# One-bank PSUM tiles in two feed-forward layers, and a planner whose lengths are distances between starts

## The chip, the cores and the metric

The kernel runs on one core of a Trainium2 chip. The metric is the device time of one execution in microseconds (us). Before the change the median of three runs is 803.41 us (802.49 to 804.92).

## The reference

Attention over 2 batches of 8 heads, 768 positions of 64 elements, in which a query sees only the keys that fall into its own hash bucket (signs of six projections). Its output, 1536 tokens of 512, goes through two feed-forward layers:

```python
attn_out = _attn_ref(q, k, v, proj)                      # softmax(mask(q k^T / 8)) v
x = attn_out.transpose(0, 2, 1, 3).reshape(1536, 512)
h = x @ w_in;  x = (h - tanh(h)) @ w_out                 # 512 -> 2048 -> 512
g = x @ w_gate                                           # 512 -> 1536
return (g * sigmoid(g) * (x @ w_val)) @ w_out2           # 1536 -> 512
```

All inputs are float32.

## The kernel before

**Precision and tiling.** Every operand of a matmul is split into a high and a low part (`split_g`, `split_w`, `x_split`), and three products of parts make one product: a *product* or an *output group* is an operation of six matmuls on TensorE (PE). The tokens go in two halves of 768 (`sb` 0 and 1), and a half in two blocks of 384 columns (`TB`).

**Seven products per unit.** A unit (`products`, L818) multiplies one pair of 128-row blocks of a weight matrix with one half of the tokens by a scheme of Strassen's kind: seven products in place of eight, P0 to P6 below, in the order of the table `PRODUCTS` (L808). Products accumulate in PSUM *banks*; a bank holds 512 float32 per partition and the core has eight. A unit uses both banks of a tile `s_t[z]` of shape [128, 2, 512] (z alternates from unit to unit), and a third bank out of a ring of four (`RING`, L813), which are the two banks of the tile `t`, also [128, 2, 512], and the one-bank tiles `x` and `h`. In the unit's order:

- P0 writes bank 0 of `s`; ScalarE (ACT) copies it out (`snap`, L830).
- P1 writes bank 1 of `s`; ACT copies it out.
- P2 writes the ring's bank; VectorE (DVE) adds the first copy (`add`, L833), and the activation follows.
- P3 adds to bank 0; ACT copies it out.
- P4 adds to bank 1; DVE adds the last copy into the bank (L833), ACT takes tanh or sigmoid (L791, L798), DVE works on (`tt`, L779), and in two of the three kinds of unit ACT and DVE make the high and the low part from that bank (L784, L779).
- P5 adds to bank 0; DVE reads it (L833).
- P6 adds to bank 0; activation and split follow.

Units are interleaved: the last products of one stand between the first of the next. Between products stand output groups (`out_group`, L882; matmuls L904), each into the ring's next bank; ACT or DVE copies the result out (L914, L915, L917, L928, L933), and for three or four results together GpSimd (POOL) issues a transfer that adds them to an accumulator (L941 in SBUF, L950 in memory).

**Weights.** They arrive as 64-bit words through two raw buffers (L271, SyncE's queue), are converted by three DVE operations per chunk (L273, L276, L279), combined (L305, L307) and split (L285, L287, L322, L324).

**Order of the work.** The order is not the program's: `Plan` (L65) holds each operation with its possible engines and a length on each, the keys that it reads and writes, a due time and a latency. `Plan.order` is a list scheduler: an engine that is free takes the ready operation with the earliest due time; an operation with two engines goes to the second when that one is free and `alt` allows. What depends on an operation becomes ready at its end plus `LAT` = 0.14 us (PE 0.25, transfers their own `lat`). Lengths of operations that were declared after the attention are multiplied by `SAFE` = 1.05. POOL and DVE operations with `port=BOTH` exclude each other. The resulting order is emitted, engine by engine, once (L1013 to the end of the function). The planner's keys are per bank: `("s", z, 0)` and `("s", z, 1)` are different things to it, as are `("t", 0)` and `("t", 1)`.

**Waits.** The tile layer below the kernel follows who touches which *tile* and puts in the semaphore waits. For the two-bank tiles of the kernel before it treats the tile as one: an access to one bank waits for earlier accesses of other engines to the other bank.

**Stages.** Attention fills the span to about 240 us, with first products of the layers in its last part; layer 1 (8 pairs of blocks) lasts to about 530 us, layer 2 (6 pairs, gate and value) to the end. In the attention the two-bank tiles are used whole: `s` for scores of 768 keys (L653, L662, L664), `t` for six transposes (L682, L688).

Of the kernel before, what the change touches and what calls it, by code (L numbers as in the profile page):

```python
# [21 lines left out]
TB = 384  # L22
# [42 lines left out]
class Plan:  # L65
# [120 lines left out]
def lsh_attention_moe_kernel(ctx: ExitStack, tc: tile.TileContext, qT, kT, vP, proj, cst, wts, out):  # L186
# [96 lines left out]
    def split_w(dst, src, rk, wk, n, due, late=False):  # L283
        hi, lo = dst
        op({"ACT": 0.19 + n / 1175}, lambda e: e.activation(out=hi, in_=src, func=ACTF.Copy),  # L285
           r=rk, w=[wk + (0,)], due=due, late=late)
# [31 lines left out]
    def declare_out(name, f, due, after):  # L318
        wk = ring("wo", NWO)
        convert(order_c[name, f], f_t, [("f", 0)], due - OLEAD, after)  # L320
        hi, lo = wo_t[wk[1]][:, 0, :], wo_t[wk[1]][:, 1, :]
        op({"ACT": 0.63}, lambda e: e.activation(out=hi, in_=f_t, func=ACTF.Copy),  # L322
           r=[("f", 0)], w=[wk + (0,)], due=due - 6)
# [454 lines left out]
    def tt(dst, dk, a, ak, b, bk, alu, due, port):  # L778
        op({"DVE": dve(TB), "POOL": pool(TB)} if port else {"DVE": 0.56}, lambda e: e.tensor_tensor(out=dst, in0=a, in1=b, op=alu),  # L779
           r=[ak, bk], w=dk, due=due, alt=ALT, port=BOTH * port)  # L780

    def split_g(key, src, sk, due, psum):
        (hi, hk, h1), (lo, lk, l1) = g_slot(), g_slot()
        op({"ACT": 0.52}, lambda g: g.activation(out=hi, in_=src, func=ACTF.Copy), r=[sk], w=[hk] + h1, due=due)  # L784
        tt(lo, [lk] + l1, src, sk, hi.bitcast(F32), hk, ALU.subtract, due + 0.6, not psum)
        gh[key] = hi, lo, [hk, lk]


    def block_tanh(key, src, sk, due, psum, keep, spare=None):
        t, tk, t1 = spare or t_slot(1)  # L790
        op({"ACT": 0.51}, lambda e: e.activation(out=t, in_=src, func=ACTF.Tanh), r=[sk], w=[tk] + t1, due=due)  # L791
        d, dk = (src, sk) if keep else (t, tk)
        tt(d, [dk], src, sk, t, tk, ALU.subtract, due + 0.6, not psum)
        split_g(key, d, dk, due + 1.2, keep and psum)

    def block_silu(key, src, sk, due, psum, keep, spare=None):
        t, tk, t1 = t_slot(2)
        op({"ACT": 0.51}, lambda e: e.activation(out=t, in_=src, func=ACTF.Sigmoid), r=[sk], w=[tk] + t1, due=due)  # L798
        tt(t, [tk], src, sk, t, tk, ALU.mult, due + 0.6, not psum)
# [12 lines left out]

    RING = [(("t", 0), t_t[0][:, 0, :]), (("t", 1), t_t[0][:, 1, :]), (("x", 0), x_t[0]), (("h", 0), h_t[0])]  # L813

    def bank_slot():
        return RING[ring("bank", len(RING))[1]]

    def products(name, i, sb):  # L818
# [5 lines left out]
        bkeys = [("s", z, 0), None, ("s", z, 1)]  # L824
        banks = [s_t[z][:, 0, 0:TB], None, s_t[z][:, 1, 0:TB]]
        (c0, k0, f0), (c1, k1, f1), (c2, k2, f2) = c_slot(), c_slot(), c_slot()
        block = {"in": block_tanh, "gate": block_silu, "val": block_val}[name]

        def snap(dst, dk, bank, bk, due):
            op({"ACT": 0.49}, lambda e: e.activation(out=dst, in_=bank, func=ACTF.Copy), r=[bk], w=dk, due=due)  # L830

        def add(dst, dk, bank, bk, c, ck, due):
            op({"DVE": 0.56}, lambda e: e.tensor_tensor(out=dst, in0=bank, in1=c, op=ALU.add), r=[bk, ck], w=[dk], due=due)  # L833

        def product(n):
            xn, wn, bi, first = PRODUCTS[n]
            if bi == 1:
                bkeys[1], b = bank_slot()
                banks[1] = b[:, 0:TB]
            bank, bk = banks[bi], bkeys[bi]  # L840
# [5 lines left out]
            def mm(e):  # L846
                m = 0
                for k in range(2):
                    for wpart, xpart in terms:
                        e.matmul(  # L850
                            out=bank, lhsT=w[:, wpart, wi * 256 + k * 128:wi * 256 + k * 128 + 128],
                            rhs=x_at(sb, xn, xpart, k), start=first and m == 0, stop=m == 5, skip_group_check=True,
# [29 lines left out]
    def out_group(layer, i, sb, j):  # L882
# [8 lines left out]
        gs = [gh[layer, i, sb, t, f] for f in range(2)]  # L891
        k, ps = bank_slot()
        ps = ps[:, 0:size]

        def mm(e):
            c = 0
            for f in range(2):
                w = wo_t[wks[f][1]]
                for wpart, gpart in terms:
                    if layer == 1:  # L900
                        lhs, rhs = w[:, wpart, m * 128:m * 128 + 128], gs[f][gpart]
                    else:
                        lhs, rhs = gs[f][gpart][:, m * 128:m * 128 + 128], w[:, wpart, :]
                    e.matmul(out=ps, lhsT=lhs, rhs=rhs, start=c == 0, stop=c == 5)  # L904
                    c += 1
# [5 lines left out]
        if layer == 1 and i in (0, NP1 - 1):  # L911
            if i == 0:
                op({"DVE": dve(TB), "ACT": 0.5}, lambda g:
                   g.activation(out=acc_at(sb, j), in_=ps, func=ACTF.Copy) if g is nc.scalar else  # L914
                   g.tensor_copy(acc_at(sb, j), ps), r=[k], w=[("acc", sb, j)], due=e, late=True)  # L915
            else:
                op({"DVE": 0.57}, lambda g: g.tensor_tensor(  # L917
                    out=acc_at(sb, j), in0=ps, in1=acc_at(sb, j), op=ALU.add,
                ), r=[k, ("acc", sb, j)], w=[("acc", sb, j)], due=e, late=True)
        elif layer == 2 and i == NP2 - 1:  # L920
# [6 lines left out]
            at_, key = stages["last"][m]  # L927
            op({"DVE": dve(DM)}, lambda g: g.tensor_tensor(out=at_(), in0=ps, in1=at_(), op=ALU.add), r=[k, key], w=[key], due=e)  # L928
            op({"SP": 0.5}, lambda g: g.dma_start(out=out[sb * S + j * 128:sb * S + j * 128 + 128, :], in_=at_()), r=[key], w=[], due=e)
        else:  # L930
            at_, key, first = stage(layer, m)
            op({"ACT": 0.18 + size / 1200, "DVE": dve(size)}, lambda g, at_=at_:
               g.activation(out=at_(), in_=ps, func=ACTF.Copy) if g is nc.scalar else g.tensor_copy(at_(), ps),  # L933
               r=[k], w=[key] + first, due=e, late=layer == 2, alt=EALT)
            if m == 0:
                stages[layer, "at"] = at_
            if m == n - 1:
                at_ = stages[layer, "at"]
                keys = [key[:3] + (c,) for c in range(n)]
                if layer == 1:  # L940
                    op({"POOL": 1.0}, lambda g, at_=at_: g.dma_start(out=acc_at(sb, 4 * t, 4), in_=at_(4), accum_op=ALU.add),  # L941
                       r=keys + aks, w=aks, due=e + 1, lat=5.0, late=True)
                else:
# [5 lines left out]
                    else:  # L949
                        op({"POOL": 1.0}, lambda g, at_=at_: g.dma_start(out=o, in_=src(at_), accum_op=ALU.add),  # L950
                           r=keys + [ok], w=[ok], due=e + 1, lat=5.0)
        if layer == 1 and i == NP1 - 1 and j == 7:
# [128 lines left out]
```

## Time and profile before

| | |
|---|---|
| median of three runs | 803.41 us |
| the profiled execution | 803.86 us, span 802.1 us |
| PE, matmuls | 766.6 us busy, 96% of the span |
| PE, weight loads (beside matmuls) | 661.5 us, 82% |
| DVE | 589.4 us, 73% |
| ACT | 466.8 us, 58% |
| POOL | 359.7 us, 45% |
| granted TensorE clock | 1.00 in every slice |
| transfers | 104.23 MB, mean 130 GB/s |

A matmul's row is longer than the time to the next matmul, because matmuls are pipelined; how fast PE goes is read from how long a run of matmuls takes as a whole. A weight load (PEld) belongs to each matmul and is issued by the same queue, so its waits are PE's waits.

### The profile page before, as it was taken

Reading aid. Unit: us, or ns where it says so; the run is one execution under the profiler, and the core shown is the slowest. Engines: PE = TensorE matmul, PEld = TensorE weight load, DVE = VectorE, ACT = ScalarE, POOL = GpSimd, SP = SyncE. Lnnn points to the kernel's source line nnn. Section 1 sums busy time; section 2 is a strip of 40 time slices with the busy share of each in tenths; the row PEclk is TensorE's granted clock in tenths of the full one; section 3 lists DMA queues with packets and bytes.
Section 4 is the critical chain, followed back from the end, with each engine's and each line's share of the span. In section 5 each row is a group of like instructions: output and inputs, shape, how many; then the busy total and the mean of one; then the engine's idle time right before and its main releaser. Section 6 shows DMA issues by size and latency. Waiting matters only on the chain.

```text
span 802.1 us, 12309 instructions
## 1 busy us (share of the span) xinstructions
PE 766.6 (96%) x4332; PEld 661.5 (82%) x4332; DVE 589.4 (73%) x1038; ACT 466.8 (58%) x906; POOL 359.7 (45%) x384
## 2 busy tenths in 40 slices
PE   5999999999999999999999999989989999999997
PEld 3766666666668889999999999989979898989996
DVE  6877777787698966786777668777765876877444
ACT  4787787786666754666545545554544455555530
POOL 4655567744475341343323454735245532344121
PEclk9999999999999999999999999999999999999999
DMA  7655444553222143777776761324327567666675
GB/s 213 161 131 139 109 133 115 124 134 74 73 66 93 53 117 94 165 189 177 178 171 161 157 142 47 86 79 158 120 73 149 128 150 158 121 155 132 119 167 187
DMA packets 38717, 104.23 MB, mean 130 GB/s; under 512 B 4704, under 2 KB 10080, under 8 KB 38656
## 3 DMA queue, kind: packets, MB, share of 16 engines
q1 hardware_dynamic: 28288, 71.06, 29.0%
q0 software_dynamic: 9904, 31.59, 22.9%
q10 hardware_dynamic: 464, 0.80, 0.4%
q8 instruction: 34, 0.56, 0.3%
q14 instruction: 27, 0.22, 0.1%
HBM read 49.17 MB, written 18.87 MB: 85 GB/s over the span
## 4 chain that ended last, share of the span: by engine, by line
PE 76%; DVE 11%; DMA 4%; ACT 3%; issue 3%; POOL 2%; SPq 0%; DVEq 0%; ACTq 0%; POOLq 0%
PE s L850 26%; PE t L904 13%; PE x L706 7%; PE t L682 7%; PE s L653 7%; PE h L904 6%; PE x L904 4%; DMA raw<-in_w 3%; DVE m L662 2%; PE x L850 2%; PE t L850 1%; ACT ct L664 1%; DMA acc<-ct 1%; DVE ct L779 1%; DVE op L779 1%
## 5 line engine op out<-in xcount | busy, mean ns | idle before, releaser
L850 PE MATMUL s<-x,wi 128*128 128x384 f32 x1200 | 235.1, 337 | 6.4 <-DVE ct L833 2.1
L850 PEld LDWEIGHTS s<-x,wi 128*128 128x128 f32 x1200 | 209.1, 188 | 18.6 <-DVE ct L833 4.0
L662 DVE TENSOR_REDUCE m<-s 128x1 f32<-128x768 f32 x96 | 89.3, 951 | 29.3 <-PE s L653 28.7
L671 POOL TENSOR_SCALAR ct<-ct,r 128x768 f32<-128x768 f32 x96 | 94.1, 988 | 33.4 <-DVE r L670 29.2
L664 ACT ACTIVATE ct<-s,m 128x768 f32<-128x768 f32 x96 | 85.8, 896 | 20.6 <-DVE m L662 19.7
L653 PE MATMUL s<-op 128*128 128x384 f32 x384 | 88.9, 366 | 6.7 <-ACT ct L664 6.4
L830 ACT ACTIVATE ct<-s 128x384 f32<-128x384 f32 x120 | 58.1, 490 | 58.6 <-PE s L850 58.1
L682 PEld LDWEIGHTS t<-csb,ct 128*128 128x128 f32 x576 | 64.4, 141 | 31.2 <-issue 18.7
L682 PE MATMUL t<-csb,ct 128*128 128x128 f32 x576 | 81.6, 278 | 5.2 <-POOL ct L671 1.7
L904 PE MATMUL t<-op,wo 128*128 128x384 f32 x384 | 77.0, 338 | 4.8 <-DVE acc L917 1.5
L653 PEld LDWEIGHTS s<-op 128*128 128x128 f32 x384 | 66.5, 195 | 17.5 <-ACT ct L664 15.3
L904 PEld LDWEIGHTS t<-op,wo 128*128 128x128 f32 x384 | 66.9, 188 | 7.8 <-DVE acc L917 2.1
L706 PE MATMUL x<-pt,v 128*64 128x384 f32 x384 | 69.0, 495 | 0.0
L287 POOL TENSOR_TENSOR wi<-fs,wi 128x512 fp32r<-128x512 f32 (+1 forms) x37 | 57.1, 1553 | 24.1 <-ACT wi L285 18.0
L904 PE MATMUL t<-wo,op 128*128 128x512 f32 x264 | 67.5, 393 | 0.0
L688 ACT ACTIVATE pt<-t 128x768 f32<-128x768 f32 x59 | 47.9, 811 | 29.7 <-PE t L682 28.6
L324 POOL TENSOR_TENSOR wo<-f,wo 128x512 fp32r<-128x512 f32 x17 | 22.4, 1316 | 75.1 <-ACT wo L322 70.9
L904 PEld LDWEIGHTS t<-wo,op 128*128 128x128 f32 x264 | 48.9, 188 | 8.2
L850 PE MATMUL s<-op,wi 128*128 128x384 f32 x240 | 48.2, 337 | 1.8 <-DVE ct L779 1.6
L706 PEld LDWEIGHTS x<-pt,v 128*64 128x64 f32 x384 | 24.7, 136 | 28.4 <-issue 28.4
L285 ACT ACTIVATE wi<-fs 128x512 fp32r<-128x512 f32 (+1 forms) x60 | 41.5, 701 | 10.4 <-DVE fs L305 4.0
L779 POOL TENSOR_TENSOR ct<-ct 128x384 f32<-128x384 f32 x20 | 20.6, 1029 | 59.9 <-ACT ct L791 31.0
(164 smaller groups left out, 1378.8 us busy)
## 6 DMA issues: line engine op xcount, KB each, us to landing
raw<-in_w SPq DMA_DIRECT2D x68, 512.0 KB, 3.9
acc<-ct POOLq DMA_DIRECT2D x24, 768.0 KB, 6.0
out<-acc POOLq DMA_DIRECT2D x16, 768.0 KB, 7.8
op<-raw SPq DMA_DIRECT2D x42, 192.0 KB, 3.0
op<-f SPq DMA_DIRECT2D x56, 96.0 KB, 2.5
v<-in_v SPq DMA_DIRECT2D x8, 384.0 KB, 3.2
out<-acc SPq DMA_DIRECT2D x4, 768.0 KB, 4.1
acc<-out SPq DMA_DIRECT2D x4, 768.0 KB, 4.5
```

What stands on the lines that cost most here:

```text
L285: op({"ACT": 0.19 + n / 1175}, lambda e: e.activation(out=hi, in_=src, func=ACTF.Copy), r=rk, w=[wk + (0,)], due=due, late=late)
L287: op({"POOL": pool(n), "DVE": dve(n)}, lambda e: e.tensor_tensor(out=lo, in0=src, in1=hi.bitcast(F32), op=ALU.subtract), r=rk + [wk + (0,) ...
L653: g.matmul(out=s[:, kh, 0:TB], lhsT=(b, a)[first][:, q0], rhs=ks[kh][0 if first else 1], start=first, stop=not first,)
L662: op({"DVE": 0.87}, lambda g: g.tensor_reduce(out=m, in_=sv, axis=AX.XY, op=ALU.max, negate=True), r=[sk + (0,), sk + (1,)], w=[mk], due=d ...
L664: op({"ACT": 0.9}, lambda g: g.activation(out=p.rearrange("p (a b) -> p a b", a=2), in_=sv, func=ACTF.Exp, bias=m, accum_out=sm), r=[sk + ...
L671: op({"POOL": 0.95}, lambda g: g.tensor_scalar(out=p, in0=p, scalar1=r, scalar2=1.0, op0=ALU.mult, op1=ALU.mult), r=[pk, rk], w=[pk], due= ...
L682: g.transpose(out=t_t[0][:, kt // 3, c0:c0 + 128], in_=p[:, kt * 128:(kt + 1) * 128], identity=ident)
L688: op({"ACT": 0.75, "DVE": 0.87}, lambda g: g.activation(out=dst, in_=src, func=ACTF.Copy) if g is nc.scalar else g.tensor_copy(dst, src), ...
L706: g.matmul(out=x[r, :], lhsT=v[:, kt, r], rhs=pt_t[ptks[e][1]][:, kt, :], start=(kt == 0), stop=(kt == NKT - 1), tile_position=(0, 64 * e),)
L830: op({"ACT": 0.49}, lambda e: e.activation(out=dst, in_=bank, func=ACTF.Copy), r=[bk], w=dk, due=due)
L850: e.matmul(out=bank, lhsT=w[:, wpart, wi * 256 + k * 128:wi * 256 + k * 128 + 128], rhs=x_at(sb, xn, xpart, k), start=first and m == 0, st ...
L904: e.matmul(out=ps, lhsT=lhs, rhs=rhs, start=c == 0, stop=c == 5)
```

## The change

Three things change.

1. In the layers each of the six banks of `s` and `t` becomes a tile of its own. The attention still uses two-bank tiles. When the last operation of the attention that touches such a tile has been emitted, its pool is closed (`narrow`) and two tiles [128, 512] are opened in its place. Operations look their bank up when they are emitted (`bank_at`, `now`).
2. The planner's lengths become the distance from one operation's start to the next one's start on the same engine: for DVE (n+65)/960 us in place of (n+151)/960 - 0.01, for ACT 0.07 + n/1200 in place of figures from 0.49 to 0.52 us for 384 columns, for POOL 0.13 + n/457 in place of 0.16 + n/457, for the conversions 0.34 and 0.60 us in place of 0.43 and 0.69. `LAT`, `SAFE`, the due times and all other constants stay.
3. The accumulating transfers: in layer 1 POOL's issue 0.87 us in place of 1.0 and a latency of 6.0 us in place of 5.0, in layer 2 1.3 in place of 1.0 and 7.5 in place of 5.0.

`pool(n)` is also used by operations on the first batch's attention output, declared within the attention (384 columns: 0.970 in place of 1.000 us).

```diff
@@ Plan
+        self.banks = {}
 ...
+        self.banks[n] = {("t", 0) if k[0] == "t" else k[:2] for k in (*r, *w) if k[0] in ("s", "t")}
@@ lsh_attention_moe_kernel
-    s_t = tiles(ctx, "s", 2, [128, 2, 512], space=PSUM)
-    t_t = tiles(ctx, "t", 1, [128, 2, 512], space=PSUM)
...
-    late = {}
+    wide = {k: ExitStack() for k in (("t", 0), ("s", 0), ("s", 1))}
+    t_t = tiles(wide["t", 0], "t", 1, [128, 2, 512], space=PSUM)
+    s_t = [tiles(wide["s", z], "s%d" % z, 1, [128, 2, 512], space=PSUM, side=("left", "right")[z])[0] for z in range(2)]
+    late = {("x", 0): x_t[0], ("h", 0): h_t[0]}
...
-    W_TS, W_STT = 0.43, 0.69
+    W_TS, W_STT = 0.34, 0.6
...
     def pool(n):
-        return 0.16 + n / 457
+        return 0.13 + n / 457
     def dve(n):
-        return (n + 151) / 960 - 0.01
+        return (n + 65) / 960
+    def act(n):
+        return 0.07 + n / 1200
...
-        op({"ACT": 0.52}, lambda g: g.activation(out=hi, in_=src, func=ACTF.Copy), r=[sk], w=[hk] + h1, due=due)
+        op({"ACT": act(TB) + 0.03}, lambda g: g.activation(out=hi, in_=now(src), func=ACTF.Copy), r=[sk], w=[hk] + h1, due=due)
...
-        op({"ACT": 0.51}, lambda e: e.activation(out=t, in_=src, func=ACTF.Tanh), r=[sk], w=[tk] + t1, due=due)
+        op({"ACT": act(TB) + 0.02}, lambda e: e.activation(out=t, in_=now(src), func=ACTF.Tanh), r=[sk], w=[tk] + t1, due=due)
...
-    RING = [(("t", 0), t_t[0][:, 0, :]), (("t", 1), t_t[0][:, 1, :]), (("x", 0), x_t[0]), (("h", 0), h_t[0])]
+    RING = [("t", 0), ("t", 1), ("x", 0), ("h", 0)]
+    def bank_at(key, size):
+        return lambda: late[key][:, 0:size]
+    def now(ap):
+        return ap() if callable(ap) else ap
+    def narrow(key):
+        wide[key].close()
+        keys = [("t", 0), ("t", 1)] if key[0] == "t" else [key + (0,), key + (1,)]
+        for k in keys:
+            late[k] = tiles(ctx, "b%s%d%d" % (*key, k[-1]), 1, [128, 512], space=PSUM, side="right")[0]
...
-        banks = [s_t[z][:, 0, 0:TB], None, s_t[z][:, 1, 0:TB]]
+        banks = [bank_at(bkeys[0], TB), None, bank_at(bkeys[2], TB)]
...
-            op({"ACT": 0.49}, lambda e: e.activation(out=dst, in_=bank, func=ACTF.Copy), r=[bk], w=dk, due=due)
+            op({"ACT": act(TB)}, lambda e: e.activation(out=dst, in_=bank(), func=ACTF.Copy), r=[bk], w=dk, due=due)
...
-            op({"DVE": 0.56}, lambda e: e.tensor_tensor(out=dst, in0=bank, in1=c, op=ALU.add), r=[bk, ck], w=[dk], due=due)
+            op({"DVE": dve(TB) + 0.01}, lambda e: e.tensor_tensor(out=now(dst), in0=bank(), in1=c, op=ALU.add), r=[bk, ck], w=[dk], due=due)
...
-                    op({"POOL": 1.0}, lambda g, at_=at_: g.dma_start(out=acc_at(sb, 4 * t, 4), in_=at_(4), accum_op=ALU.add),
-                       r=keys + aks, w=aks, due=e + 1, lat=5.0, late=True)
+                    op({"POOL": 0.87}, lambda g, at_=at_: g.dma_start(out=acc_at(sb, 4 * t, 4), in_=at_(4), accum_op=ALU.add),
+                       r=keys + aks, w=aks, due=e + 1, lat=6.0, late=True)
...
     order, first_late = plan.order()
+    last = {}
+    for i, (n, e, _) in enumerate(order):
+        for key in plan.banks.get(n, ()) if n < plan.n_first else ():
+            last[key] = i
+    ends = {i: key for key, i in last.items()}
     with tc.manual_schedule():
-        for n, e, _ in order[:first_late]:
+        for i, (n, e, _) in enumerate(order[:first_late]):
             plan.ops[n][1](eng[e])
+            if i in ends:
+                narrow(ends[i])
```

The same pattern (a looked-up bank, `act(...)` or `dve(...)` as the length) is applied to the other layer operations in `split_w`, `declare_out`, `tt`, `block_silu` and `out_group`.

## Rows read from the trace of the kernel before

**Rows 1.** Page, part 1: engine, busy us (share of the span), instructions.
```profile
PE 766.6 (96%) x4332; PEld 661.5 (82%) x4332; DVE 589.4 (73%) x1038; ACT 466.8 (58%) x906; POOL 359.7 (45%) x384
```
**Rows 2.** Busy time by stretches: length, engines' busy us (instructions), granted clock, DMA, GB/s.
```profile
240.50:300.00 59.50, 56.97 (x326) 50.21 (x325) 49.56 (x77) 38.11 (x75) 28.27 (x23) 1.00 0.30 86
300.00:500.00 200.00, 197.70 (x1119) 193.23 (x1119) 146.81 (x262) 110.57 (x230) 72.57 (x65) 1.00 0.62 148
500.00:610.00 110.00, 104.03 (x551) 96.04 (x550) 79.91 (x141) 55.86 (x108) 56.81 (x46) 1.00 0.39 112
610.00:798.00 188.00, 185.75 (x953) 169.06 (x951) 126.55 (x223) 87.05 (x169) 62.21 (x54) 1.00 0.65 144
```
**Rows 3.** The chain that ended last, in order of time: start us, us, what.
```profile
311.11 2.08 PE t L904 x12
...
614.98 7.49 DMA raw<-in_w
...
787.30 2.73 PE t L904 x12
```
**Rows 4.** Waits of PE's weight loads, 240 to 802 us: us, times, longest.
```profile
PEld s L850 <- DVE ct L779: 4.5, 9, 1.0
PEld s L850 <- DVE ct L833: 4.0, 4, 1.9
PEld s L850 <- ACT ct L830: 3.4, 5, 1.1
PEld s L850 <- DVE op L779: 3.2, 3, 1.6
...
PEld t L904 <- DVE acc L917: 2.1, 2, 1.4
PEld s L850 <- ACT op L784: 1.9, 8, 0.2
PEld t L904 <- DVE op L779: 1.7, 2, 1.0
PEld t L904 <- ACT ct L791: 1.0, 1, 1.0
PEld t L904 <- ACT acc L914: 1.0, 1, 1.0
PEld s L850 <- DVE s L779: 0.9, 2, 0.5
PEld t L904 <- DVE t L779: 0.8, 1, 0.8
```
**Rows 5.** Timeline about 586 us: start, us, engine, line, operation [idle before <-releaser].
```profile
584.42 1.26 PE L850 MATMUL s<-x,wi 128*128 128x384 f32 x6
...
585.72 0.57 DVE L779 TENSOR_TENSOR s<-s,ct 128x384 f32<-128x384 f32 x1 [0.84 <-PE s L850]
586.32 0.56 DVE L833 TENSOR_TENSOR ct<-s,ct 128x384 f32<-128x384 f32 x1
...
587.43 0.56 DVE L779 TENSOR_TENSOR op<-s,op 128x384 fp32r<-128x384 f32 x1 [0.56 <-ACT op L784]
...
588.04 0.65 PEld L850 LDWEIGHTS s<-x,wi 128*128 128x128 f32 x4 [1.64 <-DVE op L779]
```
**Rows 6.** Timeline of DVE about 624 us, operations without idle time between them.
```profile
623.43 0.69 DVE L276 SCALAR_TENSOR_TENSOR fs<-raw,fs 128x512 uint32<-128x512 uint32 x1
...
624.03 0.55 DVE L779 TENSOR_TENSOR ct<-s,ct 128x384 f32<-128x384 f32 x1
...
624.50 0.55 DVE L833 TENSOR_TENSOR ct<-s,ct 128x384 f32<-128x384 f32 x1
```
**Rows 7.** Page, part 6: transfers' issues, count, KB each, us to landing.
```profile
raw<-in_w SPq DMA_DIRECT2D x68, 512.0 KB, 3.9
acc<-ct POOLq DMA_DIRECT2D x24, 768.0 KB, 6.0
out<-acc POOLq DMA_DIRECT2D x16, 768.0 KB, 7.8
```

More of the change, by code (lines that the diff above doesn't have):

```diff
@@ L284, in split_w @@
         hi, lo = dst
-        op({"ACT": 0.19 + n / 1175}, lambda e: e.activation(out=hi, in_=src, func=ACTF.Copy),
+        op({"ACT": act(n)}, lambda e: e.activation(out=hi, in_=src, func=ACTF.Copy),
            r=rk, w=[wk + (0,)], due=due, late=late)
@@ L321, in declare_out @@
         hi, lo = wo_t[wk[1]][:, 0, :], wo_t[wk[1]][:, 1, :]
-        op({"ACT": 0.63}, lambda e: e.activation(out=hi, in_=f_t, func=ACTF.Copy),
+        op({"ACT": act(512)}, lambda e: e.activation(out=hi, in_=f_t, func=ACTF.Copy),
            r=[("f", 0)], w=[wk + (0,)], due=due - 6)
@@ L778, in tt @@
     def tt(dst, dk, a, ak, b, bk, alu, due, port):
-        op({"DVE": dve(TB), "POOL": pool(TB)} if port else {"DVE": 0.56}, lambda e: e.tensor_tensor(out=dst, in0=a, in1=b, op=alu),
+        op({"DVE": dve(TB), "POOL": pool(TB)} if port else {"DVE": dve(TB) + 0.01}, lambda e: e.tensor_tensor(out=now(dst), in0=now(a), in1=b, op=alu),
            r=[ak, bk], w=dk, due=due, alt=ALT, port=BOTH * port)
@@ L797, in block_silu @@
         t, tk, t1 = t_slot(2)
-        op({"ACT": 0.51}, lambda e: e.activation(out=t, in_=src, func=ACTF.Sigmoid), r=[sk], w=[tk] + t1, due=due)
+        op({"ACT": act(TB) + 0.02}, lambda e: e.activation(out=t, in_=now(src), func=ACTF.Sigmoid), r=[sk], w=[tk] + t1, due=due)
         tt(t, [tk], src, sk, t, tk, ALU.mult, due + 0.6, not psum)
@@ L837, in product @@
             if bi == 1:
-                bkeys[1], b = bank_slot()
-                banks[1] = b[:, 0:TB]
+                bkeys[1] = bank_slot()
+                banks[1] = bank_at(bkeys[1], TB)
             bank, bk = banks[bi], bkeys[bi]
@@ L850, in mm @@
                         e.matmul(
-                            out=bank, lhsT=w[:, wpart, wi * 256 + k * 128:wi * 256 + k * 128 + 128],
+                            out=bank(), lhsT=w[:, wpart, wi * 256 + k * 128:wi * 256 + k * 128 + 128],
                             rhs=x_at(sb, xn, xpart, k), start=first and m == 0, stop=m == 5, skip_group_check=True,
@@ L891, in out_group @@
         gs = [gh[layer, i, sb, t, f] for f in range(2)]
-        k, ps = bank_slot()
-        ps = ps[:, 0:size]
+        k = bank_slot()
+        ps = bank_at(k, size)
         def mm(e):
@@ L903, in mm @@
                         lhs, rhs = gs[f][gpart][:, m * 128:m * 128 + 128], w[:, wpart, :]
-                    e.matmul(out=ps, lhsT=lhs, rhs=rhs, start=c == 0, stop=c == 5)
+                    e.matmul(out=ps(), lhsT=lhs, rhs=rhs, start=c == 0, stop=c == 5)
                     c += 1
@@ L912, in out_group @@
             if i == 0:
-                op({"DVE": dve(TB), "ACT": 0.5}, lambda g:
-                   g.activation(out=acc_at(sb, j), in_=ps, func=ACTF.Copy) if g is nc.scalar else
-                   g.tensor_copy(acc_at(sb, j), ps), r=[k], w=[("acc", sb, j)], due=e, late=True)
-            else:
-                op({"DVE": 0.57}, lambda g: g.tensor_tensor(
-                    out=acc_at(sb, j), in0=ps, in1=acc_at(sb, j), op=ALU.add,
+                op({"DVE": dve(TB), "ACT": act(TB)}, lambda g:
+                   g.activation(out=acc_at(sb, j), in_=ps(), func=ACTF.Copy) if g is nc.scalar else
+                   g.tensor_copy(acc_at(sb, j), ps()), r=[k], w=[("acc", sb, j)], due=e, late=True)
+            else:
+                op({"DVE": dve(TB)}, lambda g: g.tensor_tensor(
+                    out=acc_at(sb, j), in0=ps(), in1=acc_at(sb, j), op=ALU.add,
                 ), r=[k, ("acc", sb, j)], w=[("acc", sb, j)], due=e, late=True)
@@ L927, in out_group @@
             at_, key = stages["last"][m]
-            op({"DVE": dve(DM)}, lambda g: g.tensor_tensor(out=at_(), in0=ps, in1=at_(), op=ALU.add), r=[k, key], w=[key], due=e)
+            op({"DVE": dve(DM)}, lambda g: g.tensor_tensor(out=at_(), in0=ps(), in1=at_(), op=ALU.add), r=[k, key], w=[key], due=e)
             op({"SP": 0.5}, lambda g: g.dma_start(out=out[sb * S + j * 128:sb * S + j * 128 + 128, :], in_=at_()), r=[key], w=[], due=e)
@@ L931, in out_group @@
             at_, key, first = stage(layer, m)
-            op({"ACT": 0.18 + size / 1200, "DVE": dve(size)}, lambda g, at_=at_:
-               g.activation(out=at_(), in_=ps, func=ACTF.Copy) if g is nc.scalar else g.tensor_copy(at_(), ps),
+            op({"ACT": act(size), "DVE": dve(size)}, lambda g, at_=at_:
+               g.activation(out=at_(), in_=ps(), func=ACTF.Copy) if g is nc.scalar else g.tensor_copy(at_(), ps()),
                r=[k], w=[key] + first, due=e, late=layer == 2, alt=EALT)
@@ L949, in out_group @@
                     else:
-                        op({"POOL": 1.0}, lambda g, at_=at_: g.dma_start(out=o, in_=src(at_), accum_op=ALU.add),
-                           r=keys + [ok], w=[ok], due=e + 1, lat=5.0)
+                        op({"POOL": 1.3}, lambda g, at_=at_: g.dma_start(out=o, in_=src(at_), accum_op=ALU.add),
+                           r=keys + [ok], w=[ok], due=e + 1, lat=7.5)
         if layer == 1 and i == NP1 - 1 and j == 7:
```

## The prediction

> **What bounds the kernel now.** I read the page's first part, the stretches, the chain, and then the waits of one engine. PE is busy for 96% of the span, and DVE, the next engine, for 73% [rows 1]. The reader is to see that this 96% is the same in every layer stretch, at a granted clock of 1.00 [rows 2], so that time can only come out of the moments in which PE stands. How many there are can't be read from busy time, because a matmul's row covers the start of the next. So I count work. In undisturbed runs 12 matmuls of 384 columns take 2.08 us (0.1733 each) and 12 of 512 columns 2.73 us (0.2275 each) [rows 3]. By the loops there are 40 units of 7 products of 6 matmuls (1680) and 128 output groups of 6 in layer 1 (768), all of 384 columns, and 72 groups of 6 in layer 2 (432) of 512 columns: 2448 x 0.1733 + 432 x 0.2275 = 424.3 + 98.3 = 522.6 us. The stretches from 240.5 to 798 us hold 2949 matmuls [rows 2], so 69 more are the attention's, at most 0.1733 each, 12 us. That is 534.6 us of work in 557.5 us: PE stands for about 22.9 us in the layers. This is the most that any better order or any fewer waits could give there.
>
> Who ends these waits is in the waits of PE's weight loads: the eleven rows shown sum to 24.5 us [rows 4], which agrees with 22.9 from the count (a weight load's wait also holds a little of its restart; factor 0.93).
>
> **The change part by part.**
>
> *The one-bank tiles.* They add no instruction. What they remove is waits between two banks of one tile. I sort [rows 4] by what each operation touches:
> - Same bank or an input, so they stay: a product after DVE's L833 (P6 after the read that follows P5) 4.0; an output group after DVE's L779 writing `op` (its own input) 1.7.
> - Other bank, so they go: products after the snapshot L830 (P1 after P0's, P4 after P3's) 3.4; after L784 and L779 writing `op` (P5 or P6 after the split of P4's bank) 1.9 and 3.2; after L779 writing `s`, 0.9; groups in `t` after L917, L791, L914 and L779 writing `t`, that is, after work on the other bank of `t`: 2.1, 1.0, 1.0, 0.8. Together 14.3.
> - Both kinds: products after L779 writing `ct`, 4.5. The read may be of P4's bank (other) or of P6's bank of the unit two before (same). I count half, 2.2.
>
> So 16.5 us of waits have a releaser on the other bank, times 0.93 is 15.4 us: the upper end. Not all of it is gained, because another releaser may stand close behind. The timeline about 586 us shows it [rows 5]. P5 (584.42) writes bank 0; DVE's multiplication on P4's bank waits for it 0.84 us although it touches bank 1; that makes the split of bank 1 late, which ends at 587.99; P6 waits for that split, 1.64 us. What P6 needs is the read L833, which ends at 586.88. So 1.11 of 1.64 us goes, two thirds. Of waits without such a neighbour all goes. I take three quarters of 15.4: **-11.5 us**. The lower end is 6 us, if only two fifths go. DVE and ACT lose waits of the same kind (the 0.84 us above); both have a quarter or more of each stretch idle [rows 2], so this counts as slack and not as time.
>
> *The lengths.* DVE's 384-column operations are planned at 0.468 x 1.05 = 0.491 us (before: 0.547 x 1.05 = 0.574). On the chip the next operation starts 0.47 us after one (624.03 to 624.50), and the conversion's second kind 0.60 us (623.43 to 624.03) [rows 6], where the planner now has 0.600 x 1.05 = 0.63 and had 0.72. So the plan stays on the safe side, with 4 to 5% to spare in place of about 20%. What depends on a DVE operation is planned 0.491 + 0.14 = 0.63 us after its start; a row of 0.55 to 0.57 us [rows 5, 6] and the start of the waiting operation just after it make about 0.61. The plan also is closer to what the engines do, so fewer operations should stand in a queue behind one whose input comes later than planned. What this is worth no row shows. Its best end: all waits that stay (4.0 + 1.7 + the other half of 4.5, 8.0 x 0.93 = 7.4 us) go. Its bad end: the plan, with DVE seemingly freer, packs more in front of the reads that P6 needs, and three or four more waits like those on L833 arise (4.0 us in 4 times [rows 4]): +4. I take **-1.5**, nearer to nothing than to either end, since waits on L833 hang on transfers (below) rather than on lengths.
>
> *The accumulating transfers.* The rows have 6.0 us in layer 1 and 7.8 in layer 2 to landing [rows 7]; the plan goes from 1.0 + 5.0 to 0.87 + 6.0, and to 1.3 + 7.5. Readers of the accumulators and staging buffers are planned later, when the data are really there. Nothing on PE waits for them directly: 0. If that cover is gone, a result copy comes 1 us later and a bank of the ring with it, which is inside the +4.
>
> *The attention.* Its own lengths stay, but for POOL's operations on the first batch's output (1.000 to 0.970) and the weights that are prepared at its end. A queue may change its order; 0, within 2 us either way. Closing the wide tiles makes a bank's first user wait for the attention's last user of both banks, as the two-bank tile did: 0.
>
> **Sum.** The profiled execution took 803.9 us: 803.9 - 11.5 - 1.5 = 790.9. It lies 0.45 us over the median of the runs shown (803.41), so on the median's scale 790.4, said as 790.5.
>
> **The rivals.**
> 1. *The plan becomes so true that nearly all idle time goes*: 15.4 + 7.4 = 22.8 us, 781. For it: 22.9 us of idle time is all there is, and the planner knew banks already, only the waits did not. Against: waits on L833 come from late weights.
> 2. *Half of the gain is given back because DVE runs behind the plan.* Spare time per operation falls from 0.574 - 0.47 = 0.10 us to 0.02 us, so a delay is no longer made up within a few operations. If P6 or P5 then waits 0.2 us more in most of the 40 units: 8 us back, 803.4 - 13 + 8 = 798.5. For it: P6 already waits for L833. Against: DVE stands for a quarter of every layer stretch [rows 2], which makes up delays too. The Trainium skill has a rule that speaks for this rival: "Perfetto Trace Analysis", section Optimizing Scalar/DVE Operations, gives an access overhead per DVE operation of about 60 ns on SBUF but about 125 ns on PSUM; by it a PSUM operation of 384 columns would take 0.525 us from start to start, more than the 0.491 planned, and six of them per unit would run 0.2 us late. This case's trace disagrees: L779 and L833 in [rows 6] read `s` in PSUM and are 0.47 us apart.
> 3. *Slower: late weights stall DVE's queue more often.* A 512 KB chunk lands after 3.9 us in the median [rows 7] and is planned at 0.5 + 3.5; one that meets an accumulating transfer landed after 7.49 us [rows 3]. The DVE conversion then waits at the head of the queue, behind it L833, and P6 waits for L833: four times, 1.0 us each [rows 4]. There are 40 accumulating transfers [rows 7]. With shorter lengths the plan puts each conversion right at the planned landing. If 24 of the 40 cost PE 1.0 us where 4 do now, that is +20: 803.4 - 11.5 + 20 = 812. It decides from 12 additional waits on. Against: a chunk's place in the queue follows its due time, which stays.
> 4. *The waits stay, or others take their place*: the tile layer still ties the new tiles, or each wait removed is followed by the next releaser. Then 803 to 804. Against: DVE's wait in [rows 5] between two banks has no other cause than the common tile.
>
> **How the numbers follow.** A measurement of this kernel can tell a change from none from about 0.3%, 2.4 us. Forecast (786 to 796): 0.60. Rival 1 (below 786): 0.14. Rival 2 (796 to 801): 0.12. Rival 4 (within 2.4 us): 0.06. Rival 3 (slower): 0.08. Faster is the first three, 0.86. The range, 781 to 801, takes in the first three but for the lowest part of rival 1; its ends are 803.4 - 22.8 and 803.4 - 6 + 4.
>
> **What would show it.** In the trace of the changed kernel PE's waits of products on L784 and on L779 writing `op`, and of groups in one bank of `t` on L917, L914 or L791, are gone, and DVE's L779 no longer waits for the product that follows in the other bank. Waits on L833 remain, some 4 us. From the first product to the last group PE takes about 544 us in place of 557. The attention ends within 2 us of where it did. If L779's, L784's and L830's other-bank waits are gone and the time is above 800, the length part is wrong by its sign; look then at DVE's waits for `raw`. If they are still there, the first step is wrong.

## The result and the profile after

The changed kernel takes 785.75 us (median of four, 784.85 to 786.83) against 803.9 us beside it: a ratio of 0.9776, 95% interval 0.9753 to 0.9798, 18 us less. 790.5 had been forecast, with a range of 781 to 801. Its profiled execution took 784.85 us with a span of 783.1 us, against 803.86 and 802.1. Two executions far out of line, one of the later kernel g2 (2629.55 us) and one of the kernel before timed beside it (855.55 us at a granted clock of 0.85), stand in no median or ratio below.

In the changed kernel's program the lines have moved: a product's matmuls are L870 (L850 before), an output group's L924 (L904), the snapshot L850 (L830), the add L853 (L833), `tt` L786 (L779), the high part L791 (L784), tanh and sigmoid L798 and L805 (L791 and L798). The one-bank tiles have names with `bs` and `bt`.

Page of the changed kernel, part 1, the line that answers to [rows 1]:

```profile
PE 754.7 (96%) x4332; PEld 660.8 (84%) x4332; DVE 601.0 (77%) x1067; ACT 470.8 (60%) x911; POOL 320.9 (41%) x350
```

Its stretches, with the columns of [rows 2]:

```profile
240.50:300.00 59.50, 58.64 (x345) 53.47 (x344) 49.85 (x83) 38.16 (x75) 22.42 (x19) 1.00 0.32 88
300.00:500.00 200.00, 200.00 (x1155) 199.72 (x1154) 160.32 (x279) 118.66 (x246) 67.48 (x63) 1.00 0.64 152
500.00:610.00 110.00, 109.31 (x586) 103.14 (x584) 92.91 (x163) 62.08 (x119) 46.86 (x38) 1.00 0.46 128
```

Busy PE is 96% as before: that share could not show the gain. The counts do: from 300 to 500 us PE gets through 1155 matmuls where it got through 1119, at the same clock of 1.00, and weight loads fill 199.72 of 200 us. The first product starts at 240.9 us (240.5 before), the last group's last six matmuls start at 777.67 and take 1.36 us by the rate of [rows 3]: 538.1 us of layers, 3.5 over the 534.6 us of work that the prediction counted, where 22.9 had been.

Waits of PE's weight loads in the changed kernel, 240 to 802 us, without those of the attention's lines and without 0.6 us of `issue` that stand in both kernels; they answer to [rows 4]:

```profile
PEld bs L870 <- DVE ct L853: 1.9, 2, 1.0
PEld bs L870 <- DVE ct L786: 1.3, 1, 1.3
...
PEld h L924 <- ACT ct L798: 0.6, 1, 0.6
```

Every group that had a releaser on the other bank is gone, and of those classed as staying most is gone too: 24.5 us (26.6 with four small rows that [rows 4] leaves out) have become 3.8. What goes on in a place like [rows 5] the timeline of the changed kernel shows about 568 us (start, us, engine, line, operation):

```profile
567.45 0.56 DVE L853 TENSOR_TENSOR bs<-bs,ct 128x384 f32<-128x384 f32 x1
...
568.04 0.57 DVE L786 TENSOR_TENSOR bs<-bs,ct 128x384 f32<-128x384 f32 x1
...
568.76 0.49 ACT L791 ACTIVATE op<-bs 128x384 fp32r<-128x384 f32 x1
569.04 0.53 PEld L870 LDWEIGHTS bs<-x,wi 128*128 128x128 f32 x3
569.21 0.51 PE L870 MATMUL bs<-x,wi 128*128 128x384 f32 x2
569.28 0.56 DVE L786 TENSOR_TENSOR op<-bs,op 128x384 fp32r<-128x384 f32 x1
```

DVE adds, multiplies and splits P4's bank (a weight split stands between the last two), while P5 of the same unit starts at 569.21 in the unit's other bank, before the split of P4's bank has begun. What the common tile does to the same operations, e2 shows below.

The same is seen from DVE. Waits of DVE for PE, of the kernel before (240 to 802 us):

```profile
DVE op L779 <- PE s L850: 16.1, 14, 1.7
...
DVE ct L779 <- PE s L850: 6.0, 6, 2.3
```

and of the changed kernel:

```profile
DVE bs L853 <- PE bs L870: 22.7, 17, 3.5
DVE ct L853 <- PE bs L870: 16.0, 16, 2.3
...
DVE ct L786 <- PE bs L870: 5.0, 8, 1.2
```

The split (`op` written by `tt`) reads what DVE and ACT have made and needs nothing of PE's newer products; 14 times it waited for one, 16.1 us in all. There is no such line after. The waits of L853 are the ordinary ones of an add for its product.

### The profile page after: what moved, and what is told of

It reads as the page before. It is cut to its first block, busy times and chain, and to the rows that moved or that the text cites. A ratio compares the mean times of both kernels' runs of the same rounds, so it can differ in the third digit from the quotient of the medians.

```text
span 783.1 us, 12307 instructions
## 1 busy us (share of the span) xinstructions
PE 754.7 (96%) x4332; PEld 660.8 (84%) x4332; DVE 601.0 (77%) x1067; ACT 470.8 (60%) x911; POOL 320.9 (41%) x350
## 4 chain that ended last, share of the span: by engine, by line
PE 63%; DVE 4%; DMA 3%; issue 0%; ACT 0%; DVEq 0%
PE bs L870 29%; PE bt L924 15%; PE h L924 8%; PE x L924 5%; DMA raw<-in_w 3%; PE x L870 2%; PE bt L870 2%; PE h L870 1%; DVE fs L283 1%; DVE fs L286 1%; PE x L713 1%; DVE pt L695 0%; DVE ct L786 0%; DVE f L283 0%; DVE fs L280 0%
## 5 line engine op out<-in xcount | busy, mean ns | idle before, releaser
L870 PE MATMUL bs<-x,wi 128*128 128x384 f32 x1200 | 232.2, 335 | 1.1 <-DVE ct L853 1.1
L870 PEld LDWEIGHTS bs<-x,wi 128*128 128x128 f32 x1200 | 210.6, 188 | 6.3 <-DVE ct L853 1.9
L689 PEld LDWEIGHTS t<-csb,ct 128*128 128x128 f32 x576 | 63.8, 140 | 32.7 <-issue 19.2
L850 ACT ACTIVATE ct<-bs 128x384 f32<-128x384 f32 x120 | 58.9, 491 | 50.0 <-PE bs L870 49.6
L660 PEld LDWEIGHTS s<-op 128*128 128x128 f32 x384 | 65.1, 192 | 20.2 <-ACT ct L671 18.7
L924 PE MATMUL bt<-op,wo 128*128 128x384 f32 x384 | 76.3, 334 | 0.0
L924 PE MATMUL bt<-wo,op 128*128 128x512 f32 x264 | 67.8, 393 | 0.0
L924 PEld LDWEIGHTS bt<-op,wo 128*128 128x128 f32 x384 | 67.4, 188 | 0.1
L294 POOL TENSOR_TENSOR wi<-fs,wi 128x512 fp32r<-128x512 f32 (+1 forms) x26 | 39.5, 1522 | 45.7 <-ACT wi L292 45.7
L924 PEld LDWEIGHTS bt<-wo,op 128*128 128x128 f32 x264 | 48.9, 188 | 7.9
L786 POOL TENSOR_TENSOR ct<-ct 128x384 f32<-128x384 f32 x19 | 19.6, 1034 | 81.3 <-ACT ct L805 48.8
L961 POOL DMA_DIRECT2D acc<-ct x24 | 21.1, 878 | 70.3 <-ACT ct L953 36.2
L870 PE MATMUL bs<-op,wi 128*128 128x384 f32 x240 | 47.9, 335 | 0.9 <-DVE ct L786 0.9
```

What stands on the lines that cost most here:

```text
L660: g.matmul(out=s[:, kh, 0:TB], lhsT=(b, a)[first][:, q0], rhs=ks[kh][0 if first else 1], start=first, stop=not first,)
L689: g.transpose(out=t_t[0][:, kt // 3, c0:c0 + 128], in_=p[:, kt * 128:(kt + 1) * 128], identity=ident)
L850: op({"ACT": act(TB)}, lambda e: e.activation(out=dst, in_=bank(), func=ACTF.Copy), r=[bk], w=dk, due=due)
L870: e.matmul(out=bank(), lhsT=w[:, wpart, wi * 256 + k * 128:wi * 256 + k * 128 + 128], rhs=x_at(sb, xn, xpart, k), start=first and m == 0, ...
L924: e.matmul(out=ps(), lhsT=lhs, rhs=rhs, start=c == 0, stop=c == 5)
```

## The experiments

Each kernel's median, and its ratio to the kernel before, timed beside it on the same chip:

| kernel | tiles | lengths | accumulating transfers | median us | ratio, 95% interval |
|---|---|---|---|---|---|
| changed | one bank | new | new | 785.75 | 0.9776 (0.9753 to 0.9798) |
| e1 | one bank | old | old | 785.4 | 0.9782 (0.9767 to 0.9797) |
| e2 | two banks | new | new | 811.9 | 1.0110 (1.0094 to 1.0126) |
| e3 | one bank | new | old | 796.8 | 0.9919 (0.9902 to 0.9936) |
| e4 | only `s` cut | new | new | 796.0 | 0.9923 (0.9898 to 0.9948) |
| g1 | one bank | new, SAFE 1.06 | new | 792.0 | 0.9860 (0.9841 to 0.9878) |
| g2 | one bank | new, weights 6.5 us | old | 785.5 | 0.9775 (0.9747 to 0.9803) |
| g3 | two banks | new, SAFE 1.25 | new | 813.7 | 1.0134 (1.0114 to 1.0154) |
| g4 | one bank | old | new | 790.8 | 0.9848 (0.9830 to 0.9865) |
| h1 | one bank | new, weights 6.5 us | new | 786.6 | 0.9789 (0.9774 to 0.9804) |
| h2 | one bank | old, weights 6.5 us | new | 789.1 | 0.9829 (0.9810 to 0.9847) |
| h3 | two banks | old, SAFE 1.06 | old | 802.3 | 0.9990 (0.9980 to 0.9999) |
| h4 | two banks | new, SAFE 1.06 | new | 819.4 | 1.0199 (1.0184 to 1.0215) |

**Kernels with the same order.** The planner knows banks and not tiles, so kernels that differ in their tiles alone get the same order. Their traces bear this out: every engine has the same operations in the same sequence in the kernel before and in e1 (DVE 1038 of them), in the changed kernel, e2 and e4 (1067), and in g1 and h4 (1063). Within each of these three sets the waits are the only difference, and they can be compared operation by operation.

**One part at a time: e1 and e2.** e1 is the changed kernel with every length and latency put back:

```diff
-    W_TS, W_STT = 0.34, 0.6
+    W_TS, W_STT = 0.43, 0.69
-        return (n + 65) / 960
+        return (n + 151) / 960 - 0.01
...
```

> One-bank tiles as in the change, but all of the planner's lengths and latencies as before the change. Waits theory (the waits between two banks of one tile were most of PE's idle time): 788 to 793 us, and in the waits of PE's weight loads the products after L784 and after L779 writing op are gone. Lengths theory (the plan's lengths did most of it, the waits were only where a wrong plan showed): 798 to 804 us. Joint theory (each half alone brings little, since a wait removed is followed by another one): 797 to 803 us here and also with the lengths alone.

e2 is the kernel before with the new lengths and latencies, the same lines in the other direction.

> All of the change's lengths and latencies, but the two-bank tiles of before throughout. Waits theory: 799 to 806 us, waits between two banks still sum to some 14 us or more. Lengths theory: 786 to 791 us. Joint theory: 797 to 803 us.

The tiles alone give the whole gain, and the lengths and latencies alone make the kernel slower by 9 us. The joint theory and the lengths theory fall. The waits theory holds in direction and in its rows, but both times lie outside its ranges: e1 is faster than 788 to 793, e2 slower than 799 to 806. At one and the same order the tiles are worth 17.5 us in the old order (the kernel before to e1), 26 us in the new one (e2 to the changed kernel) and 27 us in the new one with `SAFE` 1.06 (h4 to g1). Waits of PE's weight loads in e1, 240 to 820 us:

```profile
PEld bs L870 <- DVE ct L853: 3.5, 3, 1.6
...
PEld bs L870 <- DVE ct L786: 1.4, 2, 1.0
...
PEld h L924 <- issue: 0.6, 1, 0.6
PEld x L924 <- DVE op L786: 0.5, 1, 0.5
```

and the longest in e2 (its products are L853, its groups L907, `tt` L782, the high part L787):

```profile
PEld s L853 <- ACT op L787: 7.8, 14, 1.7
PEld s L853 <- DVE ct L782: 5.0, 6, 1.4
PEld s L853 <- DVE ct L836: 3.3, 4, 0.9
PEld t L907 <- DVE op L782: 2.9, 4, 0.8
...
PEld t L907 <- ACT ct L936: 2.8, 5, 1.2
...
PEld s L853 <- DVE op L782: 2.6, 4, 0.7
```

with this line among DVE's waits for PE in e2:

```profile
DVE op L782 <- PE s L853: 27.4, 18, 2.4
```

In e2 the waits between banks are longer than before: a product after L784 (there L787) waits 7.8 us in 14 times where it was 1.9 in 8, the split waits 27.4 us for PE where it was 16.1. The operations that the timeline of the changed kernel showed about 568 us stand in e2 about 590 us, in the same order:

```profile
589.58 1.00 PEld L853 LDWEIGHTS s<-x,wi 128*128 128x128 f32 x6 [1.28 <-ACT op L787]
...
591.01 0.56 DVE L782 TENSOR_TENSOR op<-s,op 128x384 fp32r<-128x384 f32 x1 [1.51 <-PE s L853]
...
591.82 0.55 DVE L836 TENSOR_TENSOR ct<-s,ct 128x384 f32<-128x384 f32 x1
...
592.42 0.65 PEld L853 LDWEIGHTS s<-x,wi 128*128 128x128 f32 x4 [0.79 <-DVE ct L836]
```

P5 waits 1.28 us for the high part of P4's bank, then the split of P4's bank waits 1.51 us for P5. The read of P5's bank (L836) stands behind that split in DVE's queue, and P6 waits 0.79 us for the read. This last wait is for P6's own bank, but it comes from the wait between banks before it; the same weight loads and the same split do not wait in the changed kernel.

**Half of the tiles: e4.** In `narrow`:

```diff
+        if key[0] == "t":
+            late.update({("t", i): t_t[0][:, i, :] for i in range(2)})
+            return
```

> The changed kernel, but only s is cut into one-bank tiles; t stays one tile of two banks. The rows of before put 5 of the 14 us of waits between banks on t. Waits theory: 789 to 792 us, with waits of groups in t after L953, L937 or L798 back on PE. Lengths theory: within 1 us of the changed kernel.

With `t` left whole 10 us of the 18 are lost. Waits of PE's weight loads in e4 (a group's matmuls are L927 there) have the groups in `t` again:

```profile
PEld t L927 <- ACT ct L956: 2.2, 3, 1.2
PEld t L927 <- DVE op L786: 2.0, 3, 0.8
...
PEld t L927 <- DVE acc L940: 1.3, 2, 0.9
...
PEld t L927 <- ACT op L791: 0.9, 2, 0.6
```

e4 has the order of the changed kernel, so these 10 us are the price of the tile `t` in this order. They are twice the 5 us that the rows of before put on `t`, which were read in the old order, and 796.0 lies above the 789 to 792 that the waits theory gave.

**The accumulating transfers: e3 and g4.** e3 puts back the four figures in the changed kernel, g4 sets them in e1:

```diff
-                    op({"POOL": 0.87}, ...  lat=6.0
+                    op({"POOL": 1.0}, ...   lat=5.0
-                        op({"POOL": 1.3}, ...  lat=7.5
+                        op({"POOL": 1.0}, ...  lat=5.0
```

> The changed kernel, but the four figures of the accumulating transfers as before (POOL 1.0 and 1.0, latency 5.0 and 5.0 us). My step (worth nothing): 785 to 787 us. Rival (the plan reads accumulators and staging buffers too early, and a copy stands in ACT's or DVE's queue): 788 us or more, with waits for DMA acc<-ct or out<-acc on DVE, ACT or SyncE longer than in the changed kernel.

> One-bank tiles, all lengths of before, and only the figures of the accumulating transfers new. If truer figures of these transfers help by themselves: 781 to 784 us. If they only matter with the shorter lengths: 784 to 787 us, as with the tiles alone (785.4). A reshuffle could also make it worse, over 788.

With the new lengths the new figures gain 11 us, with the old lengths they lose 5. Their worth has no sign of its own, and the step that put it at nothing (785 to 787 for e3) is wrong for these kernels. The rows of e3 say where most of its 11 us are; waits of PE's weight loads,

```profile
PEld bs L870 <- DVE ct L853: 10.1, 6, 2.9
```

and of DVE for weights:

```profile
DVE fs L280 <- DMA raw<-in_w: 8.3, 7, 3.3
DVE f L280 <- DMA raw<-in_w: 7.2, 3, 3.4
```

Most of it is the prediction's third rival, in a kernel next to the changed one: conversions at the head of DVE's queue wait for chunks, 15.5 us in all (9.4 in the changed kernel, 11.5 in e1), and L853 and P6 stand behind them. Five of P6's six waits, 7.1 us, come behind such a wait. The longest, 2.93 us at 522.42, comes behind two conversions that took 1.73 and 2.33 us beside operations of POOL, of which more below. The rival that e3's expectation named, longer waits for the accumulating transfers themselves, is not it: DVE's waits for `acc<-ct` are 1.0 us here and 1.1 in the changed kernel.

**Is it late weights, or the dealing of the order: g1, g2, h1, h2.** g1 changes `SAFE` from 1.05 to 1.06 (it does not scale PE's lengths). g2, h1 and h2 plan a weight chunk with 6.5 us:

```diff
-           w=first([rk]), due=due - 8, lat=3.5, after=after)
+           w=first([rk]), due=due - 8, lat=6.5, after=after)
```

> The changed kernel with SAFE 1.06 in place of 1.05: each planned length in the layers 1% longer, nothing else. It asks how much of 11 us a mere reshuffle of the order makes. Mechanism theory (the 11 us between the changed kernel and the one with the old figures of the accumulating transfers come from those figures): 784 to 788 us. Reshuffle theory (any small change of a length moves the order, and with it which weight chunks land late, by up to 10 us): could be anywhere from 783 to 797; over 789 speaks for it.

> The kernel with the old figures of the accumulating transfers (796.8 us), and with the weight chunks planned with a latency of 6.5 us in place of 3.5, about what the late ones take. Late-weights theory (its 11 us are DVE conversions that stand at the head of the queue for a chunk that lands late, so that L853 and P6 behind them are late): 784 to 789 us, PE's wait for L853 down from 10.1 to under 4 us, DVE's wait for raw from 15.5 to under 5. Rival (the accumulators' figures act by themselves): stays at 794 to 799.

> The changed kernel (785.75 us), with weight chunks planned with a latency of 6.5 us in place of 3.5. Late-weights theory: PE's wait for L853 (1.9 us) goes, 782 to 786 us. Reshuffle theory (any altered figure deals the order anew, and the changed kernel is one of the good deals): 786 to 797.

> One-bank tiles, old lengths, new figures of the accumulating transfers (790.8 us), with weight chunks planned with 6.5 us in place of 3.5. In that kernel one wait of 5.0 us on PE comes about 519 us from DVE conversions that run beside POOL's 768-column operations and take 1.9 to 2.3 us in place of 0.41 to 0.68, and not from a late chunk. Late-weights theory, in its strict form: 784 to 787 us. Port theory (that 5 us is where DVE and POOL meet): it goes only if the new order keeps them apart; 786 to 792, and the time follows whether rows of over 1.5 us for L283 or L286 stand before P6's read.

g2 meets the late-weights theory: 796.8 becomes 785.5, DVE has no wait for raw left in its list, and PE's wait for L853 falls to this:

```profile
PEld bs L870 <- DVE ct L853: 3.2, 3, 2.2
```

g1 shows the other side: 1% on all lengths but PE's costs 6 us, by the reshuffle theory's mark (over 789). h1 brings nothing (786.6 against 785.75, and PE's wait for L853 is 4.6 us where it was 1.9), so the strict form falls there; h2 gains 1.7 us, outside 784 to 787. Some of P6's waits have another origin, which g4 shows best. Its timeline about 514 us, conversions of DVE and the large operations of POOL beside them:

```profile
514.22 2.07 POOL L370 TENSOR_TENSOR x<-ct,x 128x768 fp32r<-128x768 f32 x1 [0.84 <-ACT x L368]
514.52 2.32 DVE L283 SCALAR_TENSOR_TENSOR fs<-raw,fs 128x512 uint32<-128x512 uint32 x1
516.25 2.24 POOL L370 TENSOR_TENSOR x<-acc,x 128x768 fp32r<-128x768 f32 x1
516.76 2.28 DVE L286 SCALAR_TENSOR_TENSOR f<-raw,f 128x512 uint32<-128x512 uint32 x1
...
520.63 0.50 PEld L870 LDWEIGHTS bs<-x,wi 128*128 128x128 f32 x2 [4.96 <-DVE ct L853]
```

A conversion that takes 0.68 us alone takes 2.3 beside POOL's operation and ends 0.55 us after it; L853 is late, and P6 waits 4.96 us. That is not yet the whole loss against e1, because e1 has three waits for L853 of its own (3.5 us). While PE stands, its granted clock falls; the stretches of g4, with the columns of [rows 2]:

```profile
519.90:526.70 6.80, 5.42 (x15) 4.72 (x16) 5.91 (x12) 2.62 (x5) 0.00 (x0) 0.50 0.42 154
526.70:533.50 6.80, 6.80 (x36) 6.12 (x35) 4.20 (x7) 3.96 (x8) 0.00 (x0) 1.00 0.24 77
```

At a granted clock of 0.50, the lower of its two levels (1.2 and 2.4 GHz), PE gets through 15 matmuls, and through 36 in an equal time behind. The waits of the layers are 9.4 us in g4 and 6.6 in e1, which is 2.6 us more by the factor 0.93; half of the 4.9 us in which PE does not wait in the slow stretch is 2.5. Together, as an estimate, that is 5.1 of the 5.4 us between the two kernels.

In h1 the same is seen at 514 us, where P6 waits 2.93 us:

```profile
514.08 2.02 POOL L375 TENSOR_TENSOR acc<-acc 128x768 f32<-128x768 f32 x1
514.32 2.07 DVE L280 TENSOR_SCALAR fs<-raw 128x512 uint32<-128x512 uint32 x1
...
519.78 1.01 PEld L870 LDWEIGHTS bs<-x,wi 128*128 128x128 f32 x6 [2.93 <-DVE ct L853]
```

So P6's remaining wait has two sources, a late chunk and a conversion that is held beside POOL. In e1, e3, g1, g2, g4, h1 and the changed kernel each wait of PE for L853 over 0.3 us, but for one of 0.86 us in g2, has one of the two in DVE's queue in the 9 us before it. Which of them strikes depends on the deal of the order. In h2 no conversion of L283 or L286 over 1.5 us stands there, and its 789.1 us are many small waits (the longest 2.1 us, a group after a weight split); the port theory's mark does not explain that kernel.

**Two-bank tiles: g3, h3, h4.** g3 and h4 are e2 with `SAFE` 1.25 and 1.06, h3 is the kernel before with 1.06.

> The kernel with the change's lengths and the two-bank tiles (811.9 us), with SAFE 1.25 in place of 1.05, so that DVE's lengths in the layers are again what they were before the change (0.468 x 1.25 = 0.585 us for 384 columns). Spare-time theory (with two-bank tiles the plan's spare time per operation covered part of the waits that it does not know; the shorter lengths took it away): back to 799 to 805 us. Rival (it was the changed proportions between engines, or a reshuffle): 807 us or more.

> The kernel before the change (two-bank tiles, old lengths), SAFE 1.06 in place of 1.05. It asks how far a reshuffle alone moves a kernel with two-bank tiles. If the kernel before was a typical deal: 798 to 812 us with an equal chance of either side; if it was a lucky one: 806 to 815. With one-bank tiles the five kernels so far lie at 785 to 797; if the waits theory holds, this one is over 797.

> Two-bank tiles with the change's lengths and figures (811.9 us at SAFE 1.05, 813.7 at 1.25), SAFE 1.06. If shorter lengths cost the two-bank kernel some 9 us by themselves: 808 to 816 us. If those were two bad deals: under 806.

h3 moves by 1 us: the kernel before was no unlucky deal that any change would have bettered. The spare-time theory falls with g3 as far as DVE goes: DVE's old lengths come back and 813.7 us stay (POOL's lengths are longer there than before, 1.21 us in place of 1.05 for 384 columns). Three deals with two-bank tiles and the new lengths lie at 811.9, 813.7 and 819.4, the last outside its range of 808 to 816, the two with the old lengths at 803.4 and 802.3. So the slowdown is no single deal. It goes through the waits for the common tiles, since e2 and h4 lose it, and more, when at the same order the tiles alone are changed; which of the lengths makes it was not tried and stays open.

## Why the prediction was right, and where its sizes were off

**The bound and its cap held.** 22.9 us of idle PE in the layers were counted; 19.4 of them went (557.5 to 538.1 us, where 544 was forecast), nothing of the attention did (0.4 us later). The signs that were named are there: the waits between banks are gone, and waits on L853 remain, 1.9 us in place of some 4.

**The tiles: right mechanism, too small.** -11.5 us had been taken, with 15.4 as the upper end; alone they give 803.4 x (1 - 0.9782) = 17.5 us (16.3 to 18.7). The kernel before and e1 have the same order, so the steps can be held against e1 wait by wait.

The prediction took off a quarter for releasers close behind, after the example of [rows 5], where P6 still needed a read that ended at 586.88. No such releaser stood behind: at the operations that made up the 14.3 us on another bank, PE does not wait at all in e1. The place of [rows 5] in e1 shows why:

```profile
569.01 0.56 DVE L786 TENSOR_TENSOR bs<-bs,ct 128x384 f32<-128x384 f32 x1
...
569.74 1.20 PE L870 MATMUL bs<-x,wi 128*128 128x384 f32 x6
...
570.98 0.56 DVE L853 TENSOR_TENSOR ct<-bs,ct 128x384 f32<-128x384 f32 x1 [1.42 <-PE bs L870]
571.46 0.55 DVE L786 TENSOR_TENSOR op<-bs,op 128x384 fp32r<-128x384 f32 x1
...
571.65 0.71 PEld L870 LDWEIGHTS bs<-x,wi 128*128 128x128 f32 x4
```

DVE's multiplication no longer waits for P5, so it does not stand ahead of the read L853 when P5 ends. The read comes 0.04 us after P5's end (before, 0.64 us), and P6 does not wait: 1.64 of 1.64 us went, and not 1.11.

The prediction also put 8.0 us of [rows 4] down as staying. In e1 5.4 us of these kinds are left (3.5 + 1.4 + 0.5), although those waits are for the same bank or for an input. One of them shows the reason. An output group at 285.65 us of before waits 1.04 us for a split, and this split had itself waited for a group in the other bank of `t`:

```profile
285.04 0.56 DVE L779 TENSOR_TENSOR op<-t,op 128x384 fp32r<-128x384 f32 x1 [1.60 <-PE t L904]
```

In e1 neither waits. So the sentence that failed is the one on DVE and ACT: their waits between banks were said to count "as slack and not as time". A delay of DVE by a wait for PE can come back to PE as a lawful wait a few operations on, as here, in [rows 5] and in e2 about 590 us. How much of the whole came this way no run separates.

All waits of the layers, with the small rows that [rows 4] leaves out and with `issue`, went from 27.2 to 6.6 us in e1. The 20.6 us between are 19.2 by the prediction's own factor 0.93, and PE's layers are 18.8 us shorter in e1; they start 0.8 us later.

The size also depends on the order: the eight kernels with all six banks cut, the changed one among them, lie at 785 to 797 us, the five with two-bank tiles at 802 to 819. The two sets don't overlap; e1 and the changed kernel are at the good end of theirs, where PE has almost no idle time left in the layers.

**The lengths: -1.5 predicted, no sign of their own measured.** With one-bank tiles the new lengths cost 11 us beside the old figures of the transfers (e1 785.4, e3 796.8) and gain 5 beside the new ones (g4 790.8, changed 785.75). Lengths and figures together give nothing: e1 and the changed kernel have ratios of 0.9782 and 0.9776 to the kernel before, with intervals that overlap nearly wholly. Where the tiles stay whole the two together cost 9, 10 and 16 us (`SAFE` 1.05, 1.25 and 1.06). The reasoning that a truer length makes a better order has no support here: the changed kernel is a good deal among its neighbours, which lie at 785 to 797 us. The bounds of the step, -7 to +4, were too narrow on the bad side for e3's 11 us.

**The accumulating transfers: 0 predicted.** The two measured effects, -11 and +5 us, are those of a reshuffle, and they hang on DVE's queue, not on readers of the accumulators: on late chunks, as the third rival described, and on conversions held beside POOL, which no rival named.

**The rivals, and luck.** 785.75 us lies in the range of 781 to 801, but just outside the forecast's own stretch (786 to 796, chance 0.60) and in that of the first rival (below 786, 0.14). That rival (the plan so true that nearly all idle time goes, 781 us) has nearly the right amount, but for another reason: the idle time went by the tiles alone. That the changed kernel is a good deal was luck; g1 and e3, which differ from it by 1% on the planned lengths and by four planned figures, take 792.0 and 796.8 us. The second (8 us given back by DVE behind the plan) did not happen: the waits of PE that are left sum to 3.8 us. The third is real in e3, with 11 us in place of 20. The fourth fell.

## What to carry to other kernels

When a scheduler works with finer resources than the layer that puts in the waits (here banks against tiles), look for waits whose two ends touch different parts of one tile, on every engine; those on engines that are not the bound make the bound's remaining waits, so don't count only the last link. Where a change leaves the planner's inputs as they are, the order stays too, and two traces can be compared wait by wait; this shows what a wait cost where a list of waits alone does not. A change of a planner's figures has to be judged over several neighbouring figures: 1% on all lengths but PE's moved this kernel by 6 us.

## What the runs showed of the hardware

A DVE conversion of 128x512 words that takes 0.41 to 0.68 us took 1.9 to 2.3 us in g4 and h1 when a 128x768 operation of POOL ran beside it, and ended 0.55 us (L283, L286) or 0.29 us (L280) after that operation. This was seen for L283 and L286, which read two SBUF tensors, and for L280, which reads one. The Trainium skill's page "SBUF — State Buffer" describes, in its section Who interferes with whom, a port pair that the two engines share and that one of them holds for a whole instruction, DVE too where it has two SBUF inputs and POOL reads SBUF; the rows of L283 and L286 agree with that. By the same section an instruction with at most one SBUF input contends only in VectorE's two-port modes. Whether L280 runs in such a mode no row says outright; for it speaks that in g4 the next operation starts 0.34 us after L280 and 0.60 us after L283, both over 512 elements.

A long wait of PE cost more than its length. The granted clock fell to 0.50 from 519.9 to 526.7 us in g4, where PE had stood 4.96 us, and also in e3 (665.0 to 668.4 us, behind a wait of 2.21), in g1 (524.6 to 528.0, behind 3.53), in g2 (521.0 to 524.4, behind 2.16) and in h1 (521.2 to 524.6, behind 2.93). In each of the last four PE got through 11 matmuls in that stretch and through 19 or 20 in an equal time behind it. In the kernel before, the changed kernel, e1, e2 and e4 the granted clock stays at 1.00 through the layers; g3 and h4 have such slow stretches too.
